# VectorE's side work in a gated MLP's tiles dealt out in other portions, and the weight loads of the projection phase moved to other steps

## The chip, the cores and the metric

One core of a Trainium2 chip runs the whole kernel. The metric is the device time of one execution in microseconds (us); the median of three runs is given. Engines are called by the profile's names: PE (TensorE; PEld is its weight load), DVE (VectorE), ACT (ScalarE), POOL (GpSimd) and SP (SyncE, which issues all DMAs of this kernel, in order).

## What is computed

A transformer block whose two branches run side by side on a layer norm of x (2048 tokens, width 640):

```python
def _B_ref(x, w_gate, w_up, w_down):
    g = jnp.einsum("bsd,df->bsf", x, w_gate)
    u = jnp.einsum("bsd,df->bsf", x, w_up)
    h = _gelu(g) * u
    return jnp.einsum("bsf,fd->bsd", h, w_down)

xn = _layernorm(x, axis=-1)
return x + _A_ref(xn, A_wqkv, A_wo) + _B_ref(xn, B_w_gate, B_w_up, B_w_down)
```

`_A_ref` is attention with 32 heads of 20 and a sliding window of 256, then a product with wo. The MLP's inner width is 1728. All is float32.

## The kernel before, in words

**Precision.** A float32 operand is split into a high part (a rounded copy, made by ACT) and a low part (raw minus high, made by DVE or POOL). A product takes three matmuls: high by high, low by high, high by low.

**Phases.** Layer norm and first projections; attention with the first MLP tiles filled in between (to about 656 us); the *gate phase* (to about 857 us); the *last phase* (to the end), in which h (1728 columns) and the attention output (640) are multiplied by w_down and wo, stacked as nine "quads" of 256 rows.

**Gate phase.** The inner width is cut into tiles f of 128 columns. Tiles f=6 to f=12 are done here, each in two passes of `gate_up_pair` (p=0 for tokens 0 to 1023, p=1 for the rest). A pass computes gate and up by a scheme that saves a product (sums of inputs and of weights, four accumulators pa, pb, pc, pe, in PSUM). It has 54 matmuls: pa 6, pb 9, pa 6, pc 9, pe 6, pc 9, pe 9. The second part of pc may start only when DVE has added the first part to q (`add(qp, pc_, q)`, L846, the "first qp add"), and the second part of pe after `add(qp, pe_, qp)`. Then come the gelu, the products h2 and h1 (L878) and their stores to hd (L882). At four places of a pass, `more(0)` to `more(3)`, the pass runs functions that were hung in (`extra`): more(0) and more(1) stand on DVE between the add to g1 and the first qp add, more(2) after the second qp add, more(3) after the add to g2. The next tile's splits and sums (`w_tiles`, `w_sums`) are among them. `load_gu` (L528) loads the next weights into "wr", two buffers.

**Side work.** A list of 21 jobs is done beside this (`Job`, L935; list, L970 to L974), each one a load by SP, some DVE instructions (items) and a store by SP:
- r0 to r3: a reciprocal of the softmax sums (1 item);
- t0 to t8: sums and differences of the four parts of a weight quad, written to wtd for the last phase (4 items, tile "ats");
- o0a, o0b to o3a, o3b: attention output times those reciprocals (3 and 2 items, tile "ato").

`work(cap)` (L978) makes one *visit*: it runs up to cap items of the oldest job under way, if that job's load was asked for at least three visits ago; a job without items left is stored and dropped; then one new job is loaded if fewer than two are under way:

```python
while n and going and going[0][1] <= hook[0] - 3:
    ...
if len(going) < 2 and jobs:
    job = jobs.pop(0)
    job.load()
    going.append((job, hook[0]))
```

ats and ato tiles share the tag "at" with three buffers; a load into a buffer waits on SP for the store of the job that had it. The caps per place are written out by hand in the loop over f. In the last tile (f=12) a loop (`while jobs or going: work(1)()`, L1224) does what is left, ahead of the second pass. Then come the first loads of the last phase (`load_step`, L1011, and `fetch`, L902); the last pass itself has the splits of the first quads (`quad`) and steps (`split_step`, L1025) hung into it.

**Last phase.** 80 steps: eight blocks of 256 tokens by nine quads and an end piece "e" (the last 64 rows of w_down, tile w13). Step n issues the loads for step n+4 (tag "hr", four buffers), splits the inputs of step n+2 and does `prepare(n)`, then its matmuls (L1087). Steps 0 to 13 (all of block 0, and quads 0 to 3 of block 1) are plain: 24 matmuls, 8 for "e". From step 15 on a step has 21 matmuls and a costlier split (tile "ss"), and needs the quads' t parts as well: t4 to t8 at steps 15 to 19, t0 to t3 at steps 26 to 29. After the last step of a block `drain` (L1096) adds the banks to x on DVE and stores the output.

`prepare` follows a table `tasks`: at the step named there the quad's high part is made (ACT, `high_quad`), at the next step its low part (DVE, `low_quad`). `("b", q)` is the quad as it is, `("t", q)` its sums from wtd. The quads are staged in "stg", three buffers of 640 KB, by `fetch`; b0, b2 and b3 come through "wr" and b1 through "at". Before, the fetches follow each other in the table's order: b4 ahead of step 0, b5 and b6 at steps 0 and 1, and from step 2 on one wherever a low part has been made (its buffer is free then).

The order of instructions on PE, ACT, DVE and SP is as written here, in the last phase POOL's too.

Of the kernel before, what the change touches and what calls it, by code (L numbers as in the profile page):

```python
# [60 lines left out]
def block_kernel(ctx, tc, x, wqk, wv, wgu, wdo, wdl, out):  # L61
# [730 lines left out]
    def w_tiles(raws, pool, bufs):  # L792
        g, u = raws
        gu = split(pool, g, [128, KT, 128], "wq", nc.gpsimd, bufs)
        uh = pool.tile([128, KT, 128], F32R, name="wqh", tag="wqh", bufs=bufs)
        ul = pool.tile([128, KT, 128], F32R, name="wql", tag="wql", bufs=bufs)
        hi_lo(u[:, 2:5], uh[:, 2:5], ul[:, 2:5], nc.gpsimd)
        return gu, (uh, ul)

    def w_sums(raws, sums):  # L800
        g, u = raws
        r = {i: c2.tile([128, 3 if i == 4 else 2, 128], F32, name=f"sr{i}") for i in (1, 2, 3, 4)}

        def dve(o, i, j, op=OP.subtract):
            nc.vector.tensor_tensor(out=o, in0=i, in1=j, op=op)

        def a1():
            dve(r[1], u[:, L], u[:, U], OP.add)
            dve(r[2], r[1], g[:, L])

        def a2():
            dve(r[3], g[:, L], u[:, L])
            dve(r[4][:, L], g[:, U], r[2])
            dve(r[4][:, 2], g[:, 4], u[:, 4])

        def fin(*which):
            for i in which:
                sums[i] = [c2.tile(list(r[i].shape), F32R, name=f"s{i}{n}") for n in "hl"]
                nc.scalar.activation(sums[i][0], r[i], AF.Copy)
            for i in which:  # L820
                dve(sums[i][1], r[i], sums[i][0].bitcast(F32))

        return a1, a2, lambda: fin(2, 1), lambda: fin(3), lambda: fin(4)
# [75 lines left out]
    def four(t):  # L899
        return t.rearrange("p k (h n) -> p (k h) n", h=2)  # L900

    def fetch(kind, q, where="stg"):  # L902
        if where == "wr":
            ts = [wrp.tile([128, KT, 128], F32, name="wr", tag="wr").rearrange("p k m -> p (k m)") for _ in range(2)]
            for i, t in enumerate(ts):
                nc.sync.dma_start(t, wdo[q][:, i])
            staged[kind, q] = [(t.rearrange("p (h n) -> p h n", h=2), slice(2 * i, 2 * i + 2)) for i, t in enumerate(ts)]
            return
        pool, bufs = (rp3, 3) if where == "stg" else (cp, 3)
        t = pool.tile([128, 4, HD], F32, name="stg", tag=where, bufs=bufs)  # L910
        nc.sync.dma_start(t, four(wdo[q]) if kind == "b" else wtd[q])
        if kind == "t" and q in borrow:
            staged[kind, q] = [(t[:, i:i + 1], slice(i, i + 1)) for i in range(4)]
        else:
            staged[kind, q] = [(t, slice(0, 4))]
# [8 lines left out]
    def high_quad(kind, q):  # L924
        for raw, t, dst in parts(kind, q):
            nc.scalar.activation(t[:, 0, dst], raw, AF.Copy)

    def low_quad(kind, q):
        for raw, t, dst in parts(kind, q):
            sub(t[:, 1, dst], raw, t[:, 0, dst].bitcast(F32))  # L930

    def sub(o, i, j, op=OP.subtract):
        nc.vector.tensor_tensor(out=o, in0=i, in1=j, op=op)  # L933
# [36 lines left out]
    jobs = [Job("r", 0), Job("r", 1)]  # L970
# [4 lines left out]
    going = []  # L975
    hook = [0]

    def work(cap):  # L978
        def fn():
            hook[0] += 1  # L980
            n = cap
            while n and going and going[0][1] <= hook[0] - 3:
                job = going[0][0]
                job.items.pop(0)()
                n -= 1
                if not job.items:
                    job.store()
                    going.pop(0)
            if len(going) < 2 and jobs:
                job = jobs.pop(0)  # L990
                job.load()
                going.append((job, hook[0]))
        return fn
# [17 lines left out]
    def load_step(n):  # L1011
        p, k = steps[n]
        c, t0 = p // 2, p % 2 * 256
        raw = raws[n] = cp.tile([128, 4, 128], F32, name="hr", tag="hr", bufs=4)
        flat = raw.rearrange("p a t -> p (a t)")
        if k == "e":
            for r in (0, 64):
                nc.sync.dma_start(flat[r:r + 64, 0:256], hd[NF - 1][c][:, t0:t0 + 256])
            return
        for i in range(2):  # L1020
            j = 2 * k + i
            src = hd[j][c] if j < NF - 1 else od[c][(j - NF + 1) * 128:(j - NF + 2) * 128]
            nc.sync.dma_start(flat[:, 256 * i:256 * i + 256], src[:, t0:t0 + 256])
# [153 lines left out]
    def split_later_xs(i, nxt=None):  # L1177
        def fn():
            split_xs(1, i, later[i])
            if nxt:  # L1180
                later[nxt] = load_xs(1, nxt)
        return fn
# [3 lines left out]
    def load_next(f):  # L1186
        def fn():
            raws_next[f] = load_gu(f)
        return fn

    raws_next = {NFA + 1: load_gu(NFA + 1)}
    for j, f in enumerate(range(NFA, NF - 1)):
        end = f + 1 == NF - 1
        first, second = {i: [] for i in range(4)}, {i: [] for i in range(4)}
        first[0] += carry
        if j == 0:
            first[0].append(split_later_xs(2, 4))
            first[2].append(split_later_xs(1))
            first[3].append(split_later_xs(3))
            second[0].append(split_later_xs(4))  # L1200
        if not end:
            nxt_w, sums = [], {}

            def next_tiles(j=j, raws=raws_next[f + 1]):
                nxt_w.append(w_tiles(raws, *pools[(len(sets) + j + 1) % 2]))

            first[3].append(next_tiles)
            items = w_sums(raws_next[f + 1], sums)
            second[2] += items[0:2]
            second[3].append(items[2])  # L1210
            carry = list(items[3:5])
            if f + 2 < NF - 1:
                second[3].append(load_next(f + 2))
        if j:
            for i, n in enumerate((0, 3, 1, 1)):
                first[i].append(work(n))
        if not end:
            for i, n in enumerate((1, 3, 1, 1) if j else (0, 0, 1, 1)):
                second[i].append(work(n))
        else:  # L1220
            fetch("b", 0, "wr")
        gate_up_pair(f, w, 0, first)
        if end:
            while jobs or going:  # L1224
                work(1)()
            for n in range(2):
                load_step(n)
            fetch("b", 1, "at")

            def quad(q):  # L1230
                high_quad("b", q)
                low_quad("b", q)

            second[0].append(lambda: quad(0))
            second[1].append(lambda: [split_step(0), fetch("b", 2, "wr"), load_step(2)])
            second[2].append(lambda: [split_step(1), quad(1), load_step(3)])
            second[3].append(lambda: [quad(2), fetch("b", 3, "wr")])
        stores = gate_up_pair(f, w, 1, second, end)
        if not end:
            w = nxt_w[0], sums  # L1240
# [9 lines left out]
    psn = p3.enter_context(tc.tile_pool(name="psn", bufs=1, space=PSUM, reuse_waits="tile"))  # L1250
    w13 = rp3.tile([128, 2, D], F32R, name="w13")

    tasks = {0: ("b", 3), 1: ("b", 4), 2: ("b", 5), 3: ("b", 6), 4: ("b", 7), 5: ("b", 8), 6: ("t", 4), 8: ("t", 5),
             9: ("t", 6), 10: ("t", 7), 11: ("t", 8), 12: ("t", 0), 13: ("t", 1), 20: ("t", 2), 22: ("t", 3)}
    queue = list(tasks.values())[1:]

    def prepare(n):
        if n in tasks:
            high_quad(*tasks[n])
        if n - 1 in tasks:  # L1260
            low_quad(*tasks[n - 1])
            if n > 1 and queue:
                fetch(*queue.pop(0))
        if n == 2:
            nc.scalar.activation(w13[:, 0], raw13, AF.Copy)
            sub(w13[:, 1], raw13, w13[:, 0].bitcast(F32))
        if n < 2:
            fetch(*queue.pop(0))

    fetch(*queue.pop(0))  # L1270
    for o, i in stores:
        nc.sync.dma_start(o, i)
    raw13 = rp3.tile([128, D], F32, name="xr", tag="xr")
# [2 lines left out]
    for n, (p, k) in enumerate(steps):  # L1276
        i = n % (NQD + 1)
# [62 lines left out]
```

## Time and profile before

| | us |
|---|---|
| median of three runs | 1107.2 (1105.37 to 1108.08) |
| the profiled execution | 1105.0 |
| its span | 1103.3 |
| PE busy | 1072.4 (97%) |
| DVE busy | 757.5 (69%) |
| ACT busy | 510.2 (46%) |
| POOL busy | 335.3 (30%) |
| first matmul of the gate phase's passes | about 671 |
| first matmul of the last phase | 856.7 |

The profile is of one execution. Busy time is that in which an engine executes; a matmul's end is modelled. Rows of a timeline give start, length, engine, line, operation, what is written and read, how many were merged, and in brackets the idle time ahead of it and what ended it. Rows of a table by stretch give for each engine busy time and count, then PE's granted clock, the busy share of the DMA engines and GB/s.

### The profile page before, as it was taken

The numbers are of one execution on the slowest core, as the hardware profiler recorded it, in microseconds if no ns is written. First come the engines' busy times: TensorE is split into PE (matmuls) and PEld (weight loads), VectorE is DVE, ScalarE is ACT, GpSimd is POOL, SyncE is SP. The second block draws the span as 40 slices with busy tenths as digits, with TensorE's granted clock in tenths as the row PEclk, the third lists the DMA queues.
The fourth block names the chain that finished last, engine by engine and source line by source line (L and its number), as shares of the span: only waits on it lengthen the run. The fifth ranks groups of instructions, "written<-read, shape, count | busy, mean of one in ns | idle before, by whom it ended". The sixth has DMA issues, their size and how long they took to land.

```text
span 1103.3 us, 20904 instructions
## 1 busy us (share of the span) xinstructions
PE 1072.4 (97%) x7253; PEld 858.0 (78%) x7253; DVE 757.5 (69%) x2089; ACT 510.2 (46%) x1031; POOL 335.3 (30%) x513
## 2 busy tenths in 40 slices
PE   8999999999999999999999999999995999999998
PEld 7877667666678767666666778888884999999998
DVE  7766667566666666666756636777775578888886
ACT  4434655556644556554554565233222454333332
POOL 5045624567626425644525241111110000000000
PEclk9999999999999999999999999999997999999999
DMA  5642342536443243434333225476567894343433
GB/s 203 193 135 90 104 145 86 151 110 199 131 116 94 78 119 101 135 128 128 108 112 97 63 84 186 154 243 218 208 231 272 269 302 153 108 138 118 138 123 113
DMA packets 96057, 162.30 MB, mean 147 GB/s; under 512 B 13248, under 2 KB 57920, under 8 KB 95952
## 3 DMA queue, kind: packets, MB, share of 16 engines
q1 hardware_dynamic: 95952, 160.97, 46.1%
q8 instruction: 57, 0.93, 0.4%
q14 instruction: 48, 0.39, 0.1%
HBM read 104.40 MB, written 56.23 MB: 146 GB/s over the span
## 4 chain that ended last, share of the span: by engine, by line
PE 77%; DVE 8%; DMA 7%; ACT 3%; issue 2%; SPq 1%; POOL 1%; DVEq 0%; ACTq 0%
PE ps_d L100 23%; PE ps_g L843 15%; PE ps L1087 11%; PE ps_o L515 7%; PE ps_e L493 7%; PE ps_m L441 7%; PE ps_v L100 5%; DMA hr<-hd 2%; DVE ss L933 2%; DMA hr<-od 1%; PE ps_g L100 1%; DVE junk L443 1%; DVE xr L1101 1%; ACT at L1047 1%; ACT P L495 1%
## 5 line engine op out<-in xcount | busy, mean ns | idle before, releaser
L443 DVE CUSTOM_DVE_ANT_0 junk<-ps_m,mask 128x384 bf16<-128x384 f32 (+2 forms) x512 | 271.7, 531 | 177.2 <-PE ps_m L441 135.9
L495 ACT ACTIVATE P<-ps_e 128x512 f32<-128x512 f32 (+2 forms) x384 | 197.7, 568 | 63.7 <-PE ps_e L493 57.5
L1087 PE MATMUL ps<-wb,at 128*128 128x320 f32 x999 | 156.6, 309 | 1.4 <-DVE xr L1101 1.2
L1087 PEld LDWEIGHTS ps<-wb,at 128*128 128x128 f32 x999 | 148.9, 188 | 2.3 <-issue 1.5
L501 POOL TENSOR_SCALAR_AFFINE_SELECT P<-P 128x512 f32<-128x512 f32 x128 | 84.5, 660 | 175.4 <-ACT P L495 168.5
L100 PE MATMUL ps_d<-xh,wql 128*128 128x512 f32 x430 | 129.2, 410 | 0.0
L100 PE MATMUL ps_d<-xl,wqh 128*128 128x512 f32 x430 | 128.6, 408 | 0.0
L100 PE MATMUL ps_d<-xh,wqh 128*128 128x512 f32 x430 | 128.5, 409 | 0.0
L441 PE MATMUL ps_m<-ks,qs 120*128 120x128 bf16 (+1 forms) x704 | 121.1, 275 | 3.6 <-DVE mx L443 1.9
L493 PE MATMUL ps_e<-qs,ks 122*128 122x128 bf16 (+2 forms) x704 | 113.0, 277 | 1.4 <-ACT P L495 0.8
L493 PEld LDWEIGHTS <-ks 122*128 122x128 bf16 x704 | 50.1, 98 | 54.8 <-issue 44.1
L1087 PE MATMUL ps<-wt,at 128*128 128x320 f32 x552 | 89.8, 310 | 0.8 <-DVE u L933 0.7
L100 PEld LDWEIGHTS ps_d<-xh,wql 128*128 128x128 f32 x430 | 77.9, 189 | 15.8 <-issue 2.3
L100 PEld LDWEIGHTS ps_d<-xl,wqh 128*128 128x128 f32 x430 | 78.2, 188 | 14.9 <-issue 0.6
L100 PEld LDWEIGHTS ps_d<-xh,wqh 128*128 128x128 f32 x430 | 77.8, 189 | 14.1 <-ACT xh L184 0.3
L441 PEld LDWEIGHTS <-qs 120*128 120x128 bf16 x704 | 62.1, 98 | 32.8 <-issue 14.1
L1087 PEld LDWEIGHTS ps<-wt,at 128*128 128x128 f32 x552 | 83.0, 188 | 1.8 <-DVE u L933 1.3
L515 PE MATMUL ps_o<-P,v 128*32 128x384 f32 (+2 forms) x1408 | 84.3, 386 | 0.0
L504 POOL TENSOR_SCALAR_AFFINE_SELECT P<-P 128x512 f32<-128x512 f32 x112 | 72.1, 654 | 37.3 <-ACT P L495 37.3
L515 PEld LDWEIGHTS ps_o<-P,v 128*32 128x32 f32 x1408 | 40.1, 110 | 39.5 <-issue 29.6
L224 POOL TENSOR_TENSOR pt<-r,pt 128x512 bf16<-128x512 f32 x40 | 46.7, 1169 | 79.3 <-ACT pt L223 79.2
L1047 ACT ACTIVATE at<-ss 128x512 fp32r<-128x512 f32 x59 | 37.2, 630 | 66.4 <-DVE ss L933 65.8
(179 smaller groups left out, 1700.2 us busy)
## 6 DMA issues: line engine op xcount, KB each, us to landing
hr<-hd SPq DMA_DIRECT2D x104, 128.0 KB
hd<-he SPq DMA_DIRECT2D x50, 256.0 KB
wr<-wgu SPq DMA_DIRECT2D x27, 320.0 KB
qs<-qd SPq DMA_DIRECT2D x32, 240.0 KB
ks<-kd SPq DMA_DIRECT2D x32, 240.0 KB
ats<-wdo SPq DMA_DIRECT2D x9, 640.0 KB
wtd<-ats SPq DMA_DIRECT2D x9, 640.0 KB
stg<-wtd SPq DMA_DIRECT2D x9, 640.0 KB
```

The costliest lines, as they stand in the source:

```text
L100: nc.tensor.matmul(ps, a(k), b(k), start=n == 0, stop=n == 3 * nk - 1)
L224: nc.gpsimd.tensor_tensor(out=pt[:, l, :], in0=r, in1=pt[:, 1, :], op=OP.subtract)
L441: nc.tensor.matmul(ps[:, lo:hi], lh, rhs, start=True, stop=True)
L443: nc.vector.tensor_tensor_reduce(out=junk[:, 0:n], in0=ps[:, 0:n], in1=mask[:, 384 - n:384], scale=1.0, scalar=NEG, op0=OP.add, op1=OP.max ...
L493: nc.tensor.matmul(ps[:, col:col + n], k[0:QROWS, j, kc:kc + 128], q[0:QROWS, j, q0:q0 + n], start=True, stop=True)
L495: nc.scalar.activation(pt[:, j, lo:hi], ps[:, lo:hi], AF.Exp, scale=SCALE)
L501: nc.gpsimd.affine_select(out=a, in_=a, pattern=[[0, 4], [1, 128]], compare_op=OP.is_ge, fill=0.0, base=0, channel_multiplier=-1)
L504: nc.gpsimd.affine_select(out=a, in_=a, pattern=[[0, 4], [-1, 128]], compare_op=OP.is_ge, fill=0.0, base=-1, channel_multiplier=1)
L515: nc.tensor.matmul(o[32 * j:32 * j + 32, q0:q0 + n], v[:, w0_:w0_ + 32], pt[:, j, col:col + n], start=i == 0, stop=i == len(todo) - 1, ski ...
L843: nc.tensor.matmul(ps, i, j, start=first and n == 0, stop=n == len(work) - 1, skip_group_check=True)
L1047: nc.scalar.activation(hi[:, 3:7], s, AF.Copy)
L1087: nc.tensor.matmul(ps[bank][:, 0:HD], a, b, start=bank not in begun, stop=final[p, bank] == n and j == len(work[bank]) - 1, skip_group_che ...
```

## The change

Three things. The caps of the visits are other ones; three jobs may be under way instead of two; and the loop that did the rest in the last tile is gone (an assertion stands there: nothing may be left). In the last phase the table `tasks` has most quads one or two steps later (t2 and t3 stay), and the fetches stand in a table of their own: b5 and b6 at steps 0 and 1 as before, each later one at three steps ahead of its task or when its buffer is free (one step after the task three fetches earlier), whichever is later. Worked out, the fetches stand at these steps:

| | b5 | b6 | b7 | b8 | t4 | t5 | t6 | t7 | t8 | t0 | t1 | t2 | t3 |
|---|---|---|---|---|---|---|---|---|---|---|---|---|---|
| before | 0 | 1 | 2 | 3 | 4 | 5 | 6 | 7 | 9 | 10 | 11 | 12 | 13 |
| after | 0 | 1 | 3 | 4 | 5 | 7 | 8 | 9 | 11 | 12 | 13 | 17 | 19 |

```diff
-            if len(going) < 2 and jobs:
+            if len(going) < 3 and jobs:
                 job = jobs.pop(0)
                 job.load()
                 going.append((job, hook[0]))
...
         if j:
-            for i, n in enumerate((0, 3, 1, 1)):
+            for i, n in enumerate((0, 3, 1, 2)):
                 first[i].append(work(n))
         if not end:
-            for i, n in enumerate((1, 3, 1, 1) if j else (0, 0, 1, 1)):
+            for i, n in enumerate((2, 3, 1, 1) if j else (0, 2, 1, 1)):
                 second[i].append(work(n))
         else:
             fetch("b", 0, "wr")
         gate_up_pair(f, w, 0, first)
         if end:
-            while jobs or going:
-                work(1)()
+            assert not jobs and not going
             for n in range(2):
                 load_step(n)
             fetch("b", 1, "at")
...
-    tasks = {0: ("b", 3), 1: ("b", 4), 2: ("b", 5), 3: ("b", 6), 4: ("b", 7), 5: ("b", 8), 6: ("t", 4), 8: ("t", 5),
-             9: ("t", 6), 10: ("t", 7), 11: ("t", 8), 12: ("t", 0), 13: ("t", 1), 20: ("t", 2), 22: ("t", 3)}
-    queue = list(tasks.values())[1:]
+    tasks = {0: ("b", 3), 2: ("b", 4), 3: ("b", 5), 4: ("b", 6), 5: ("b", 7), 6: ("b", 8), 8: ("t", 4), 10: ("t", 5),
+             11: ("t", 6), 12: ("t", 7), 13: ("t", 8), 14: ("t", 0), 15: ("t", 1), 20: ("t", 2), 22: ("t", 3)}
+    late = list(tasks)[2:]
+    fetch_at, ready = {}, [1] + [n + 1 for n in list(tasks)[1:]]
+    for i, n in enumerate(late):
+        fetch_at[i if i < 2 else max(n - 3, ready[i - 1])] = tasks[n]
 
     def prepare(n):
         if n in tasks:
             high_quad(*tasks[n])
         if n - 1 in tasks:
             low_quad(*tasks[n - 1])
-            if n > 1 and queue:
-                fetch(*queue.pop(0))
...
-        if n < 2:
-            fetch(*queue.pop(0))
-
-    fetch(*queue.pop(0))
+        if n in fetch_at:
+            fetch(*fetch_at[n])
+
+    fetch("b", 4)
```

## The prediction

> **What bounds the kernel now.** I read the page first, then the waits of PE, then the chain that ended last, then the stretch around the one large gap engine by engine.
>
> ```profile
> span 1103.3 us, 20904 instructions
> ...
> PE   8999999999999999999999999999995999999998
> ...
> PEclk9999999999999999999999999999997999999999
> ```
>
> TensorE is the bound: its row reads 9 in every slice but three. Slice 31 (827 to 855 us) has 5 and a granted clock of 7. The waits of PE name it:
>
> ```profile
> PE ps_g L843 <- DVE qp L846: 12.8, 1, 12.8
> ```
>
> That one wait is larger than all others of PE together. The chain through it (start, length, what):
>
> ```profile
> 832.10 3.72 DMA wtd<-ats
> 835.88 3.71 DMA ats<-wdo
> ...
> 850.64 4.19 PE ps_g L843 x9
> ```
>
> and VectorE in that time:
>
> ```profile
> 832.16 1.90 DVE L933 TENSOR_TENSOR ato<-ato,rb 128x512 f32<-128x512 f32 x3
> ...
> 838.28 1.29 DVE L933 TENSOR_TENSOR ato<-ato,rb 128x512 f32<-128x512 f32 x2 [4.22 <-DMA ato<-od]
> ...
> 841.86 2.07 DVE L933 TENSOR_TENSOR ats<-ats 128x320 f32<-128x320 f32 x4 [2.29 <-issue]
> ```
>
> Between the two passes of the last tile (f=12) the loop at L1224 empties what is left of the jobs: I count one item of t2, five of o3, four of t3, ten in all. VectorE takes its instructions in order, so the adds that PE needs (L846) stand behind ten items, of which six wait for loads that were issued only then. The load of t3 itself waited for the store of t2 (its buffer). That is the stall: not VectorE's work, but loads asked for too late.
>
> **The change part by part.**
>
> *The loop in the last tile goes.* Counted by the rule in work(): before, the visits offer 62 items and 50 are taken by the end of the last tile's first pass, because only two jobs are under way and one must be three visits old. After, with three under way and 75 offered, all 60 are done at the first visit of the second pass of f=11; the last tile has none. So the 12.8 us of waiting go, and a loss of clock behind them:
>
> ```profile
> 847.00:852.00 5.00, 1.36 (x3) 1.17 (x4) 2.58 (x4) 1.27 (x3) 0.00 (x0) 0.50 0.95 305
> ...
> 867.00:872.00 5.00, 3.96 (x27) 3.69 (x26) 1.92 (x2) 2.38 (x5) 0.00 (x0) 1.00 0.96 359
> ```
>
> ```profile
> 726.47 0.69 DVE L846 TENSOR_TENSOR qp<-ps_g,q 128x512 f32<-128x512 f32 x1
> ...
> 824.39 0.69 DVE L846 TENSOR_TENSOR qp<-ps_g,q 128x512 f32<-128x512 f32 x1 [0.58 <-PE ps_g L843]
> ...
> 856.72 14.24 PE L1087 MATMUL ps<-wb,at 128*128 128x320 f32 x96
> ```
>
> In the stretches the third number from the end is the granted clock: 0.50 behind the long gap, 1.00 around a gap of about 1 us. A pass is 54 matmuls; its first qp add comes at 726.47 and, eight passes on, at 824.39, so 12.24 us a pass, 0.227 a matmul. The 18 matmuls left behind the gap took 850.64 to 856.72 = 6.08 us instead of 4.08: 2.0 more. Together **-14.8**.
>
> *The items in other portions.* Nearly all 60 items now lie in f=7 to f=11, up to five ahead of the first qp add, where before there were at most four:
>
> ```profile
> 700.00 0.95 DVE L944 RECIPROCAL rc<-rc 128x128 f32<-128x128 f32 x1
> ...
> 711.45 1.93 DVE L933 TENSOR_TENSOR ats<-ats 128x320 f32<-128x320 f32 x4
> ...
> 724.48 1.89 DVE L933 TENSOR_TENSOR ato<-ato,rb 128x512 f32<-128x512 f32 x3
> ...
> 825.25 0.41 PEld L843 LDWEIGHTS ps_g<-xh,s4h 128*128 128x128 f32 x2
> ```
>
> An item costs 0.48 (ats), 0.64 (ato) or 0.95 (reciprocal). The add may be late by little: the one at 824.39 ends at 825.08 and PE's dependent load starts at 825.25. Second passes fit: the fullest (f=7: three ats, two ato, 2.7 us from 711.45) ends at 714.2, when its add is due (726.47 less one pass). First passes are tighter: three ato at f=8 ended at 726.37, 0.10 ahead of the add; after, f=8 has ato, reciprocal, ats (2.1 us), f=9 two ato and a reciprocal (2.2), f=10 and f=11 three ato as before, each behind larger items at visits 2 and 3 of the pass ahead. I work out lateness of 0.1 to 0.4 us in four passes. Bounds: nothing, or one ato uncovered in each of four (2.6); near the tight row, **+0.5**.
>
> *Three loads under way* share the three "at" buffers, so that seven times a load stands on SP right behind the store that frees its buffer, 3.72 us (the wtd store above). Behind it on SP stand, at worst, the next tile's weights:
>
> ```profile
> 766.90 0.82 SPq L528 DMA_DIRECT2D wr<-wgu  x2
> ...
> 780.02 0.72 ACT L92 ACTIVATE wqh<-wr 128x640 fp32r<-128x640 f32 x1
> ```
>
> They are issued 13.1 us ahead of their first reader; with 3.7 for landing 9.4 are spare. Two such pairs in one pass (second passes of f=9, f=10) block SP for 7.4 us, less than that. I take 0; the other end, all seven uncovered, is 26 (a rival below).
>
> *The last pass without its pause.* The pause also covered the first loads of the last phase.
>
> ```profile
> 831.08 0.93 SPq L882 DMA_DIRECT2D hd<-he  x2
> ...
> 844.38 2.44 SPq L1023 DMA_DIRECT2D hr<-hd  x4
> 846.87 0.43 SPq L911 DMA_DIRECT2D stg<-wdo  x1
> ...
> 862.12 1.66 SPq L1018 DMA_DIRECT2D hr<-hd  x2
> ```
>
> That was SP's queue, and this is ScalarE:
>
> ```profile
> 834.52 0.60 ACT L862 ACTIVATE q<-ps_g 128x512 f32<-128x512 f32 x1 [1.49 <-PE ps_g L843]
> ...
> 848.63 0.63 ACT L1038 ACTIVATE at<-hr 128x512 fp32r<-128x512 f32 x1 [3.43 <-DMA hr<-hd]
> 851.98 1.27 ACT L926 ACTIVATE wb<-stg 128x1280 fp32r<-128x1280 f32 x1 [1.31 <-DMA stg<-wdo]
> ...
> 868.78 0.42 ACT L1031 ACTIVATE he<-hr 128x256 fp32r<-128x256 f32 x1 [1.70 <-DMA hr<-hd]
> ```
>
> Now the hr loads go out at 832.0, right behind the hd stores. If they take as long as here (844.38 to 848.63, 4.25 us) they are there at 836.3; ScalarE's copy 0.63, VectorE's subtraction 0.69, then the qp add 0.69 make 838.3. PE ran dry at 837.8 (850.64 less 12.8), and its next matmul was due 0.1 earlier. So a wait of 0.6; or of 0.2 when the load is faster and ScalarE's order alone sets it (q from 834.52 and the gelu behind it, 0.6 each, end at 835.75). The upper end is a load as slow as the one from 862.12 to 868.78, 6.7 us: 840.7, a wait of 3.0. I take **+0.6**, by the nearest row. [...]
>
> *First steps of the last phase.* What follows is late against PE, because PE no longer waits:
>
> ```profile
> 872.08 0.41 PE L1087 MATMUL ps<-w,he 128*128 128x320 f32 x1 [1.12 <-ACT w L1265]
> 872.94 1.29 PE L1087 MATMUL ps<-w,he 128*128 128x320 f32 x7 [0.45 <-DVE w L933]
> ...
> 893.06 14.31 PE L1087 MATMUL ps<-wb,at 128*128 128x320 f32 x96 [1.23 <-DVE xr L1101]
> ```
>
> and from SP and ScalarE:
>
> ```profile
> 857.72 1.07 SPq L906 DMA_DIRECT2D wr<-wdo  x2
> ...
> 870.13 1.27 ACT L926 ACTIVATE wb<-stg 128x1280 fp32r<-128x1280 f32 x1 [0.92 <-DMA stg<-wdo]
> 871.31 0.72 ACT L1265 ACTIVATE w<-xr 128x640 fp32r<-128x640 f32 x1
> ```
>
> b1 would be issued at 834.4 and with 5.1 us (846.87 to 851.98) reach ScalarE at 839.5; copy, subtraction, g2 add, gelu, copy and half a subtraction of b2 (1.3 + 1.5 + 0.7 + 0.6 + 0.7 + 0.8) free b3's buffer at 845, 2.6 us behind step 0 (837.7 + 4.08 + 0.6 = 842.4), where it is 1.0 now. So b3, and w13 at step 4, come 1.5 us later against PE. In return w13's copy no longer stands behind b5's (870.13 to 871.31; b4, landed earlier, takes that place): -0.9. **+0.5** on the 1.57 us of waiting at step 4; ends -1.57 and +2.
>
> *Weight loads spread out.* To step 11 ten quads are fetched instead of twelve, 1.3 MB less in front of the hr loads while the DMA share is 0.96. The 1.23 us at 893.06 come from the drain's first add, which VectorE reaches late, behind a split whose hr load it awaits; I give half back, **-0.6** (0 to -1.23). The price: t7, t8, t0, t1 are now converted at steps 13 to 16, where only t0 and t1 were.
>
> ```profile
> 903.28 0.29 DVE L933 TENSOR_TENSOR ss<-hr 128x128 f32<-128x128 f32 x1 [0.51 <-DMA hr<-hd]
> ...
> 905.61 1.48 DVE L933 TENSOR_TENSOR wt<-stg,wt 128x1280 fp32r<-128x1280 f32 x1
> ...
> 911.79 0.29 DVE L933 TENSOR_TENSOR ss<-hr 128x128 f32<-128x128 f32 x1 [0.96 <-DMA hr<-od]
> ...
> 923.42 1.68 DVE L1101 TENSOR_TENSOR xr<-ps,xr 128x320 f32<-128x320 f32 x4
> ```
>
> From 911.79 to the drain at 923.42 VectorE does five splits, 2.33 us each, without a gap. Two more subtractions of 1.5 to 1.7 make 3.2; the 0.96 of DMA wait pays part, so the drain is at most 2.3 late if VectorE still starts step 13 at 903.28, and not late if earlier hr loads let it start 2 us sooner. **+0.6**.
>
> Sum: -14.8 + 0.5 + 0.6 + 0.5 - 0.6 + 0.6 = **-13.2**. The profiled execution took 1105.0 us (span 1103.3, 1.7 around it): 1091.8. The median shown is 2.2 above it, so on its scale 1107.2 - 13.2 = **1094.0**.
>
> **Rivals.**
> *The last pass still waits.* For: its hr loads now follow the stores by nothing. With the 6.7 us load: 3.0 instead of 0.6, 1096.4; if so long a gap also cost clock, up to 2.0 more, 1098.4. [...] The trace has 12.8 us with loss and 1.1 without, and nothing between.
> *All covered.* The waits at 872 and 893 vanish too: -14.8 + 0.2 - 1.57 - 1.23 = -17.4, 1089.8. For: less DMA traffic; against: b3's chain.
> *SP's queue becomes the bound (slower).* Seven store-then-load pairs at 3.72 are 26 us; were all exposed to PE through late weights of the next tile, 1094.0 + 26 = 1120. It begins to cost where the blocks of a pass exceed 9.4 us, and is a loss from about 13 us exposed. Against it: two pairs make 7.4.
> *The change moves the stall instead of removing it* (items that wait for their loads in f=8 to f=11): shortest lead of a load on its first item that I count is 8 to 10 us, against 3.7 to 7.4 needed. If so, about 1107.
>
> **How the numbers follow.** Forecast 0.63, last pass still waits 0.15, all covered 0.13, SP's queue 0.05, stall moved 0.04. The range 1089.5 to 1099.5 holds the first three and leaves the rest out. A measurement of this kernel tells about 0.3% (3.3 us) from no change: faster 0.91, within 0.03, slower 0.06.
>
> **What would show it.** Right: no wait of PE on L846 above 1 us, granted clock 1.00 throughout 820 to 860, the first L1087 matmul near 842.5, ats and ato rows only up to about 810. Wrong: waits of PE on L846 in f=8 to f=11 adding up to over 3 us, L528 issues later than 9 us, or PE waits on DVE xr around 910 of over 2 us.

## The result, and the profile after

| | before | after |
|---|---|---|
| median (lowest to highest), us | 1107.64 (1105.37 to 1108.71, 4 runs) | 1094.07 (1092.35 to 1095.3, 4 runs) |
| profiled execution, its span | 1105.0, 1103.3 | 1093.39, 1091.7 |

The ratio is 0.9879, 95% interval 0.9857 to 0.9901: faster by 1.2%. The forecast was 1094.0. The page of the kernel after:

```profile
span 1091.7 us, 20910 instructions
...
PE   8999999999999999999999999999999999999998
...
PEclk9999999999999999999999999999999999999999
```

The 5 in slice 31 and the 7 of its clock are gone. The waits of PE (line waited for: us in total, times, longest), from the top:

```profile
PE ps_t L176 <- DVE xi L159: 3.9, 4, 1.5
PE ps_m L441 <- DVE mx L443: 2.0, 6, 0.7
PE ps_m L441 <- DMA sd<-ob: 1.5, 1, 1.5
PE ps_u L387 <- DVE warm L384: 1.2, 1, 1.2
PE ps L1087 <- ACT w L1265: 1.1, 1, 1.1
PE ps L1087 <- DVE u L933: 1.1, 2, 0.7
```

The 12.8 us on L846 headed this list before. Now L846 isn't in it, and what is left in the last phase are single waits of at most 1.15 us. The chain that ended last no longer goes through the side work's wtd and ats in the last tile. It goes through the first loads of the last phase:

```profile
835.18 5.09 DMA stg<-wdo
846.99 7.06 DMA stg<-wdo
854.07 3.08 DMA hr<-hd
```

The last pass, on SP, ScalarE and VectorE:

```profile
831.83 0.93 SPq L882 DMA_DIRECT2D hd<-he  x2
833.17 1.97 SPq L1023 DMA_DIRECT2D hr<-hd  x4
```

```profile
835.77 0.62 ACT L863 ACTIVATE hr<-hr 128x512 f32<-128x512 f32 x1
836.37 0.63 ACT L1038 ACTIVATE at<-hr 128x512 fp32r<-128x512 f32 x1
```

```profile
837.03 0.69 DVE L933 TENSOR_TENSOR at<-hr,at 128x512 fp32r<-128x512 f32 x1 [0.91 <-ACT at L1038]
837.64 0.68 DVE L846 TENSOR_TENSOR qp<-ps_g,q 128x512 f32<-128x512 f32 x1
```

The loads stand right behind the stores, and ScalarE's copy of what they brought (836.37) starts when the gelu ahead of it is done, with no wait for a DMA in its brackets. The first qp add ends at 838.32, and no matmul of PE waited for it (its weight load did, 0.17 us).

**Where the time went.** Three rows cut both traces at the same work: the first DVE product of the gate phase, the first matmul of the last phase (856.72 before, 842.60 after), and the end pieces "e" of blocks 1 and 2, which are the rows ps<-w,he. Before:

```profile
662.58 0.69 DVE L765 TENSOR_TENSOR he<-ps_g,gs 64x512 f32<-64x512 f32 x1 [1.07 <-ACT gs L764]
```

```profile
907.21 1.34 PE L1087 MATMUL ps<-w,he 128*128 128x320 f32 x8
936.89 1.34 PE L1087 MATMUL ps<-w,he 128*128 128x320 f32 x8
```

After:

```profile
663.33 0.69 DVE L765 TENSOR_TENSOR he<-ps_g,gs 64x512 f32<-64x512 f32 x1 [1.07 <-ACT gs L764]
```

```profile
842.60 11.27 PE L1087 MATMUL ps<-wb,at 128*128 128x320 f32 x74
...
859.13 0.41 PE L1087 MATMUL ps<-w,he 128*128 128x320 f32 x1 [1.15 <-ACT w L1265]
859.99 1.57 PE L1087 MATMUL ps<-w,he 128*128 128x320 f32 x7 [0.45 <-DVE w L933]
...
894.54 1.34 PE L1087 MATMUL ps<-w,he 128*128 128x320 f32 x8
925.31 1.34 PE L1087 MATMUL ps<-w,he 128*128 128x320 f32 x8
```

| us | before | after | difference |
|---|---|---|---|
| ahead of the gate phase (no edit there) | 662.58 | 663.33 | +0.75 |
| gate phase | 194.14 | 179.27 | -14.87 |
| last phase, first matmul to e of block 1 | 50.49 | 51.94 | +1.45 |
| e of block 1 to e of block 2 | 29.68 | 30.77 | +1.09 |
| the rest of the span | 166.41 | 166.39 | 0.0 |

The gate phase gained 14.9 us, and the first two blocks of the last phase gave 2.5 back. In the first of these stretches a loss appears that before had not at this place (busy time and count of PE, PEld, DVE, ACT, POOL, then granted clock, DMA share, GB/s):

```profile
856.00:860.00 4.00, 2.40 (x16) 1.92 (x14) 1.31 (x3) 3.12 (x5) 0.00 (x0) 1.00 0.91 341
860.00:864.00 4.00, 4.00 (x16) 3.70 (x17) 3.95 (x4) 2.56 (x3) 0.00 (x0) 0.60 0.78 232
864.00:868.00 4.00, 4.00 (x28) 4.00 (x28) 2.09 (x2) 1.22 (x2) 0.00 (x0) 0.97 0.93 304
```

From 860 to 864 PE did 16 matmuls where 29 fit, at a clock of 0.60, behind gaps of 0.33, 1.15 and 0.45 us. By whole microseconds from 860 on the clock is 0.91, 0.50, 0.50, 0.50 and 0.89: about 3.4 us at half speed. What that cost is read from the rows: from step 4's second matmul to e1 after takes 34.55 us (from 859.99), before 33.04 (from 872.94, without a gap of 1.23 at the first drain), so 1.5 us. Before, the same place had gaps of 1.12 and 0.45 and kept its clock:

```profile
870.00:874.00 4.00, 2.43 (x15) 1.94 (x14) 3.12 (x4) 3.87 (x5) 0.00 (x0) 1.00 0.86 291
874.00:878.00 4.00, 4.00 (x29) 4.00 (x28) 2.89 (x3) 1.50 (x2) 0.00 (x0) 1.00 0.90 278
```

A second loss there is seen only in part in PE's rows. The 96 matmuls of steps 0 to 3 last from 842.60 to 857.99, 15.39 us, where before they take 14.24. At step 3 the weight loads (PEld) stand idle for 0.26, 0.55 and 0.29 us, until 853.46, 854.20 and 854.93: for the low part of that step's input and for the two low parts of b3, which VectorE makes late because ScalarE had to wait for b3's load:

```profile
851.43 0.74 ACT L926 ACTIVATE wb<-wr 128x640 fp32r<-128x640 f32 x1 [1.87 <-DMA wr<-wdo]
```

```profile
853.33 1.56 DVE L933 TENSOR_TENSOR wb<-wr,wb 128x640 fp32r<-128x640 f32 x2
```

### The profile page after: what moved, and what is told of

It reads as the page before. It is cut to its first block, busy times and chain, and to the rows that moved or that the text cites. A ratio compares the mean times of both kernels' runs of the same rounds, so it can differ in the third digit from the quotient of the medians.

```text
span 1091.7 us, 20910 instructions
## 1 busy us (share of the span) xinstructions
PE 1073.2 (98%) x7253; PEld 857.9 (79%) x7253; DVE 757.4 (69%) x2089; ACT 509.7 (47%) x1031; POOL 335.3 (31%) x513
## 4 chain that ended last, share of the span: by engine, by line
PE 78%; DVE 9%; DMA 5%; ACT 3%; issue 3%; SPq 1%; POOL 1%; DVEq 0%; ACTq 0%
PE ps_d L100 23%; PE ps_g L843 15%; PE ps L1087 12%; PE ps_o L515 7%; PE ps_e L493 7%; PE ps_m L441 6%; PE ps_v L100 6%; DVE ss L933 2%; DMA hr<-hd 1%; PE ps_g L100 1%; DVE junk L443 1%; DMA stg<-wdo 1%; DVE xr L1101 1%; ACT at L1047 1%; ACT P L495 1%
## 5 line engine op out<-in xcount | busy, mean ns | idle before, releaser
L1087 PE MATMUL ps<-wb,at 128*128 128x320 f32 x999 | 159.1, 312 | 0.6 <-DVE wb L933 0.3
L100 PEld LDWEIGHTS ps_d<-xl,wqh 128*128 128x128 f32 x430 | 78.3, 188 | 14.8 <-issue 0.6
```

The lines of the kernel that those rows point to most:

```text
L100: nc.tensor.matmul(ps, a(k), b(k), start=n == 0, stop=n == 3 * nk - 1)
L1087: nc.tensor.matmul(ps[bank][:, 0:HD], a, b, start=bank not in begun, stop=final[p, bank] == n and j == len(work[bank]) - 1, skip_group_che ...
```

## The experiments

All stretches below are cut as in the table above; "to e1" is the first matmul of the last phase to e of block 1, "e1 to e2" the next one. The part ahead of the gate phase lies between 662.6 and 667.9 in these traces, though nothing there was edited, so stretches say more than single spans. Each ratio is to the kernel before, run beside it. In pool_low the lines behind L931 are numbered three higher, and w13's copy is at L1261 to L1266 depending on the kernel.

| kernel | runs: median (range) | ratio, 95% interval | gate | to e1 | e1 to e2 |
|---|---|---|---|---|---|
| gate_only | 1094.85 (1092.98 to 1097.15) | 0.9890 (0.9873 to 0.9907) | 179.28 | 53.47 | 29.25 |
| table_only | 1105.82 (1104.31 to 1108.24) | 0.9988 (0.9977 to 0.9998) | 193.96 | 48.84 | 30.25 |
| three_only | 1100.07 (1098.5 to 1101.65) | 0.9936 (0.9919 to 0.9952) | 182.50 | 53.62 | 28.91 |
| caps_only | 1097.31 (1096.08 to 1101.57) | 0.9918 (0.9897 to 0.9938) | 183.30 | 53.71 | 29.78 |
| b1_early | 1091.8 (1090.58 to 1092.39) | 0.9862 (0.9843 to 0.9881) | 179.27 | 50.66 | 31.16 |
| w13_early | 1096.18 (1094.35 to 1096.88) | 0.9902 (0.9887 to 0.9917) | 179.22 | 54.95 | 31.30 |
| both_new | 1092.79 (1089.63 to 1093.37) | 0.9869 (0.9850 to 0.9888) | 179.22 | 48.39 | 31.16 |
| both_old | 1094.2 (1090.19 to 1094.49) | 0.9877 (0.9858 to 0.9896) | 179.62 | 52.25 | 29.26 |
| b1_w13 | 1091.58 (1090.87 to 1093.16) | 0.9848 (0.9821 to 0.9875) | 179.87 | 49.78 | 32.31 |
| pool_low | 1095.33 (1094.28 to 1097.05) | 0.9887 (0.9869 to 0.9904) | 180.02 | 49.47 | 34.33 |
| t01_late | 1094.38 (1092.37 to 1096.37) | 0.9870 (0.9850 to 0.9891) | 179.63 | 49.59 | 28.96 |

The theory: the gain is the stall of the last tile and nothing else; what is given back comes from the first steps of the last phase, whose loads the stall had covered, and from VectorE's way to the second drain. The rivals: the new table is what gains, or three loads under way (or the new caps) would have done by themselves.

### The halves alone: gate_only and table_only

gate_only is the kernel after with the old `tasks`, `queue` and `prepare`; table_only is the kernel before with the new ones.

> The other caps, three jobs under way and no loop in the last tile, but the last phase's table and fetches as before. Theory (the loop's stall and its clock loss are the whole gain; the new table only moves waits of a microsecond about): 12.5 to 15.5 us faster than before, no wait of PE on L846 above 1 us, PE waiting 1.5 to 2.5 us for w13 at step 4 and 1 to 1.5 us at the first drain, none of 1 us at the second. Rival (the spread loads are needed, since without the pause the last phase is short of DMA): only 8 to 11 us faster, with 2 to 5 us more PE waits in steps 3 to 12 than in the changed kernel.

> Only the new table and fetches of the last phase; gate phase as before with its loop. Theory: within 1.5 us of before; the 12.8 us wait of PE on L846 stays, the w13 wait shrinks by about 0.9 us and the second drain costs about 1 us more. Rival (the spread loads bring a part of the gain): 2 to 5 us faster.

gate_only has after's gate phase to 0.01 us, and after's time within the spread. Two of its waits came out otherwise than expected: 2.67 us at step 4, where 1.5 to 2.5 was said, and only 0.20 at the first drain, where 1 to 1.5 was. PE comes to that drain late itself. table_only keeps the stall:

```profile
PE ps_g L843 <- DVE qp L846: 12.3, 1, 12.3
```

So the gain is the gate phase's. The table's part is a trade: against gate_only, after is 1.53 better to e1 and 1.52 worse from e1 to e2. With the stall still there (table_only against before) it is 1.65 better and 0.57 worse, and the runs show 0.1%, just told from nothing. In gate_only PE waits longer at step 4, and the loss of clock behind it is longer too:

```profile
860.41 0.64 PE L1087 MATMUL ps<-w,he 128*128 128x320 f32 x1 [2.67 <-ACT w L1264]
```

```profile
860.00:864.00 4.00, 3.36 (x11) 3.02 (x12) 3.61 (x5) 2.86 (x5) 0.00 (x0) 0.50 0.86 256
864.00:868.00 4.00, 4.00 (x21) 4.00 (x20) 1.22 (x1) 0.96 (x1) 0.00 (x0) 0.65 0.99 298
```

### The gate phase's two parts alone: three_only and caps_only

Both are the kernel before, with its loop and its old table.

```diff
# three_only
-            if len(going) < 2 and jobs:
+            if len(going) < 3 and jobs:
# caps_only
-            for i, n in enumerate((0, 3, 1, 1)):
+            for i, n in enumerate((0, 3, 1, 2)):
-            for i, n in enumerate((1, 3, 1, 1) if j else (0, 0, 1, 1)):
+            for i, n in enumerate((2, 3, 1, 1) if j else (0, 2, 1, 1)):
```

> Before, with three jobs under way instead of two, nothing else; the loop stays, and by my count it has one item left (the last of t3), whose load was asked for a tile earlier. Theory (late loads are the stall, not the items): 12 to 15 us faster than before. Rival (the stall is VectorE's amount of work in the gate phase, which the new portions change): under 5 us faster.

> Before, with the new caps only, two jobs under way; by my count the loop has the four items of t3 left, whose load was asked for in the last tile's first pass, about 8 us ahead. Theory: 11 to 14.5 us faster, a PE wait on L846 of 0.5 to 2.5 us left. Rival (only the third load under way does it): under 8 us faster, a wait of 5 us or more left.

Each alone brings most of the gate phase's gain, and neither all of it. In the runs both missed their expectation: three_only gained 0.64% where 12 to 15 us (1.1 to 1.4%) were expected, caps_only 0.82% where 11 to 14.5 us (1.0 to 1.3%) were. Their gate phases are 11.6 and 10.8 us shorter, and both give 3.1 to 3.2 back to e1, by a wait at step 4 (2.63 and 2.02) with a lower clock behind it (0.67 from 868 to 872 in three_only, 0.57 from 864 to 868 in caps_only). three_only's waits of PE on L846 are two, 2.7 us together, and behind the first stands the very queue that the prediction had as its slower rival. SP and VectorE of three_only in f=11:

```profile
802.57 0.38 SPq L967 DMA_DIRECT2D od<-ato  x1
...
809.01 0.38 SPq L958 DMA_DIRECT2D ato<-od  x1
809.49 0.91 SPq L882 DMA_DIRECT2D hd<-he  x2
```

```profile
815.34 0.69 DVE L878 TENSOR_TENSOR he<-qp,hr 128x512 f32<-128x512 f32 x1 [4.07 <-DMA hd<-he]
...
819.23 0.69 DVE L846 TENSOR_TENSOR qp<-ps_g,q 128x512 f32<-128x512 f32 x1
```

A side-work load waits on SP for the store of its buffer, the last 3.1 us of it alone, until 809.01. The stores of the h that VectorE had finished at 802.0, in the pass before, stand behind it and go out at 809.49. VectorE needs their buffer for the next products and waits 4.07 us for them; the qp add behind it is late and PE waits 1.27. The second wait, 1.41, is in the last pass: the one item that is left starts at 838.43, its store goes out at 838.96 and the hr loads behind it only at 839.46. In caps_only the pass of the last tile has t3's four items in it. They cost nothing by themselves (2.06 us from 832.09). But the store of their result (SP, 834.17) stands ahead of the hr loads (834.60), and VectorE waits for these:

```profile
839.32 0.69 DVE L933 TENSOR_TENSOR at<-hr,at 128x512 fp32r<-128x512 f32 x1 [3.11 <-DMA hr<-hd]
```

```profile
840.67 1.22 PE L843 MATMUL ps_g<-xh,s4h 128*128 128x512 f32 x2 [2.27 <-DVE qp L846]
```

That is the prediction's rival "the last pass still waits", near its size (2.27 where 3.0 was said, and a granted clock of 0.57 from 840 to 844), in a kernel that leaves one job over. In before, three_only and caps_only, each with items left in the last tile, the wait is there; in gate_only and after, with an empty list, it is gone.

### The first steps of the last phase: b1_early, w13_early, both_new, both_old

All on the kernel after. b1_early issues b1's fetch ahead of the last tile's first pass instead of behind it. w13_early takes w13 ahead of the quads and b4's fetch behind the loads for step 4. both_new does both, both_old does both with the old table.

```diff
# b1_early
             fetch("b", 0, "wr")
+            fetch("b", 1, "at")
         gate_up_pair(f, w, 0, first)
...
-            fetch("b", 1, "at")
# w13_early, in prepare(n); w13's two lines stand ahead of the quads
+        if n == 0:
+            fetch("b", 4)
...
-    fetch("b", 4)
```

> The changed kernel, with b1 fetched ahead of the last tile's first pass instead of behind it. Theory (the last phase lost 2.5 us because its first loads are asked for too late against PE, each link waiting for the one before: b1, the subtraction of b2, b3's buffer, the stores, the loads of step 4): ScalarE's wait of 2.3 us for b1 goes, b3 is asked for 1 to 1.5 us earlier, the wait for w13 shrinks from 1.6 us to under 0.7, no clock is lost there; 1.5 to 3.5 us faster than the changed kernel. Rival (DMA throughput, not the time of asking, sets when step 4's inputs land): no change, within 0.7 us.

> The changed kernel, with b4's fetch behind step 4's loads instead of ahead of the stores, and w13's copy and subtraction ahead of b4's. Theory: 640 KB less ahead of w13 and the hr load of step 4, which land 2 us earlier or more; the wait at step 4 falls from 1.6 us to under 0.5 and the half clock behind it (1.65 us) goes: 2 to 3.5 us faster than the changed kernel. Rival (the wait only moves to b4 at step 5 or to b3 at step 3): under 1 us faster, the same sum of PE waits in steps 3 to 6.

> Both of the above. Theory: no wait of PE above 0.5 us from step 0 to the first drain, clock 1.00 throughout; 2.5 to 4 us faster than the changed kernel, some 16 to 18 faster than before. Rival (the last phase is bound by its DMA volume): as the better of the two alone or worse.

> The same two edits with the old table of the last phase. Theory (the new table costs about 1 us at the second drain, since VectorE has two more subtractions there, and gives nothing that the two edits don't): 0 to 1.1 us faster than with the new table, second drain's PE waits 0.4 instead of 1.1. Rival (spread loads matter once PE no longer pauses): 1 us or more slower than with the new table, by waits for hr loads in steps 4 to 12.

b1_early gains 1.28 to e1 (ratio 0.9862 against 0.9879, the intervals overlap). b3 goes out 1.57 us behind the first matmul of the last phase (843.65) instead of 3.27 (845.87 in after), the three waits at step 3 are gone, and e of block 0 begins 15.39 us after that matmul instead of 16.53 (15.36 before). The wait at step 4, which was expected to go, stays: the piece he lands at 855.22, and b4's copy of 1.25 us stands between it and w13's. w13_early has the longest last phase of all (252.67 us against after's 249.10), though in the runs its interval overlaps after's: b4 and the input of step 5 behind it are late instead, PE waits 2.79 us at step 5, and the clock is at 0.50 until 868. both_new has the shortest way to e1 of all, with one gap of 0.99 us and a clock of 1.00. But 2.5 to 4 us over after were expected of it, and its median is only 1.3 better; the profiled execution is the fastest of its four (1089.63, the others 1092.51 to 1093.37). both_old shows what the new table is for once b1 is early. With the old one PE waits at the first drain, which is the wait that the prediction gave half back:

```profile
PE ps L1087 <- DVE xr L1101: 2.5, 1, 2.5
```

But from e1 to e2 it is again the other way round, 29.26 against 31.16: of the 3.86 us that the new table saves in block 0, half is paid at the second drain. In the runs the two can't be told apart.

### The second drain: b1_w13, pool_low, t01_late

b1_w13 is b1_early with w13's two lines ahead of the quads, and b4's fetch where the change has it. The other two build on it: pool_low does three late subtractions on POOL, t01_late puts t0 and t1 behind the drain, and t2 and t3 a little later, so that the third block has all four.

```diff
# pool_low, in low_quad
+            if kind == "t" and q in (8, 0, 1):
+                nc.gpsimd.tensor_tensor(out=t[:, 1, dst], in0=raw, in1=t[:, 0, dst].bitcast(F32), op=OP.subtract)
# t01_late
-             11: ("t", 6), 12: ("t", 7), 13: ("t", 8), 14: ("t", 0), 15: ("t", 1), 20: ("t", 2), 22: ("t", 3)}
+             11: ("t", 6), 12: ("t", 7), 13: ("t", 8), 19: ("t", 0), 21: ("t", 1), 23: ("t", 2), 25: ("t", 3)}
```

> The changed kernel with b1 fetched ahead of the last tile's first pass, and in prepare(2) w13's copy (ScalarE) and subtraction (VectorE) ahead of b4's; b4's fetch stays where the change has it. Theory (the first steps of the last phase lose 1.57 us of waiting at step 4 because w13's copy stands behind b4's 1.27 us copy, and 1.7 us of clock behind it): with b1 early the piece he lands at 855.2, w13's copy no longer stands behind b4's, the wait at step 4 falls from 1.2 + 0.4 to under 0.4, PE's granted clock stays at 1.00 from 856 to 866 in the profile, and block 0 is some 1.5 to 3 us shorter: last phase 246 to 247, 1089 to 1091 in the runs. Rival (the wait only moves, as it did with w13 early alone): b4's copy, 0.7 later on ScalarE, and its low part on VectorE become late for step 5, PE waits 1 us or more on them, and the last phase stays at 248 to 249, 1091.5 to 1094.

> The kernel with b1 early and w13's copy ahead, and the low parts of t8, t0 and t1 (steps 14 to 16) on POOL, which does nothing in the last phase, instead of VectorE. Theory (with the new table VectorE comes late to the second drain, because these 128x1280 subtractions of 1.48 us lie in its last seven splits): VectorE reaches the drain's first add 3 to 4 us earlier against the first step, the wait of PE on m (1.49 us) goes, and from the e piece of block 1 to that of block 2 it takes 29.2 to 29.7 us instead of 32.3; last phase 246 to 246.5, 1088.5 to 1090 in the runs. Rival (the loads hr set VectorE's pace there, the subtractions only fill its waits): VectorE waits for hr instead, and the stretch stays at 31 to 32 us. Second rival: POOL's subtraction, an estimated 3.2 us from its 1.62 us for 128x640, makes VectorE's rows longer while it runs or frees the staging buffer so late that t2's or t1's load slips; then rows of at<-ss over 0.75 us show it.

> The kernel with b1 early and w13's copy ahead, and t0 and t1 behind the second drain: tasks at steps 19 and 21, t2 and t3 at 23 and 25 (t0 to t3 are needed from step 26 on). Theory: two subtractions of 1.48 us fewer ahead of the second drain, VectorE reaches it about 3 us earlier, no wait on m; from the e piece of block 1 to that of block 2 29.2 to 29.7 us instead of 32.3. The third block then has four subtractions in place of two; its stretch stays at 30.1 us if VectorE has the room (nine splits of 2.33, the drain's 5.5, four times 1.48: 32.4 us of about 30.8, so it may lose up to 1.5 at the third drain). Last phase 246 to 248, 1088.5 to 1091. Rival (hr loads set VectorE's pace): the second stretch stays at 31 to 32.

In b1_w13 both expectations hold in part. At step 4 the gaps are 0.20 and 0.44, the clock stays at 1.00, and b4 costs 0.99 a step later, as the rival said; the median lies in the rival's range. It reaches e1 2.16 us sooner than after does, and then PE waits at the second drain:

```profile
860.96 31.70 PE L1087 MATMUL ps<-wb,at 128*128 128x320 f32 x214 [0.99 <-DVE wb L933]
910.73 1.51 PE L1087 MATMUL ps<-wb,at 128*128 128x320 f32 x6 [1.49 <-ACT m L1114]
914.59 0.70 PE L1087 MATMUL ps<-wt,at 128*128 128x320 f32 x3 [0.72 <-DVE u L933]
```

From e1 to e2 it takes 32.31: 1.54 of the 2.16 are given back there, because VectorE sets that point and PE only comes to it earlier. t01_late shows it: with two subtractions of 1.48 us out of the way that stretch is 28.96, the shortest but one of the runs, and the wait on m there is gone. The next stretch (e of block 2 to e of block 3) pays: 34.44 instead of 30.13, a loss of 4.3 where at most 1.5 was expected, so the kernel as a whole gains nothing.

```profile
894.73 1.33 PE L1087 MATMUL ps<-w,he 128*128 128x320 f32 x8
923.69 1.34 PE L1087 MATMUL ps<-w,he 128*128 128x320 f32 x8
958.13 1.34 PE L1087 MATMUL ps<-w,he 128*128 128x320 f32 x8
```

```profile
943.62 1.51 PE L1087 MATMUL ps<-wb,at 128*128 128x320 f32 x6 [1.97 <-ACT m L1114]
```

So the two subtractions can be moved from one drain to the next, and whichever block has it is late. pool_low fell by its second rival, and by more than that said. POOL, then VectorE, in pool_low:

```profile
898.68 3.05 POOL L931 TENSOR_TENSOR wt<-stg,wt 128x1280 fp32r<-128x1280 f32 x1 [3.19 <-ACT wt L926]
```

```profile
898.61 0.29 DVE L936 TENSOR_TENSOR ss<-hr 128x128 f32<-128x128 f32 x1
898.82 3.06 DVE L936 TENSOR_TENSOR ss<-hr,ss 128x128 f32<-128x128 f32 x1
```

The VectorE instruction that meets POOL's takes 3.06 us instead of 0.29: it ends 0.15 us after POOL's. The other two go the same way (3.26 and 3.02 us on VectorE). Handing over 1.48 us of VectorE's work cost VectorE about 2.8 us.

The fastest of all are b1_early and b1_w13, 1091.8 and 1091.58 in the runs. They beat the kernel before, and after by some 2 us in the median; the intervals of the ratios (b1_w13 to 0.9875, after from 0.9857) still overlap. Their traces don't bear the 2 us out: from the first product of the gate phase to the end they take 427.9 and 428.7 us, after 428.4. That they are faster than after is not shown.

## Why the prediction was right, point by point

**The loop goes, -14.8.** Right, in both its parts. The gate phase is 14.87 us shorter, with nothing for two terms beside it. The last side-work item starts at 810.13, the wait of 12.8 is gone, and the 18 matmuls behind the first qp add take 4.12 us (838.48 to 842.60) instead of 6.08, at a clock of 1.00 from 820 to 860.

**Items in other portions, +0.5.** Measured 0.0: from 699.34 to 821.74 ten passes of after take 122.40 us, as ten of before do from 698.59 to 820.99. No first qp add was late enough for PE.

**SP's store-then-load pairs, 0.** Right for after. Two pairs lie in the second passes of f=9 and f=10, and the weights behind them went out at 772.16 and 799.10 instead of 766.90 and 791.38, by 5.3 and 7.7 us (0.75 of it from ahead of the gate phase), under the 9.4 that were spare. The rival built on them was sound in its mechanism: three_only shows it, through the stores of h and not through the weights.

**The last pass without its pause, +0.6.** Measured 0. The loads, issued at 833.17, were there by 836.37, in at most 3.2 us where 4.25 was taken, and ScalarE's order set the copy, as in the case that the prediction priced at 0.2. The 4.25 was a misreading: it counts from the start of four issues that keep SP busy for 2.44 us. In the chain of before the load that the copy waited for takes 2.25 us, from 846.39 on.

**First steps of the last phase, +0.5 for the waits.** Measured about +2.7, beyond the +2 that the step allowed. The waits at step 4 are 1.60 (1.15 and 0.45), as good as the 1.57 before. What failed is two things. The prediction saw b3 come late, but priced it at step 4 alone: b3 went out 3.27 us behind the first matmul instead of the 2.6 worked out, and cost 1.15 at step 3. And the step priced no clock: it was at half speed for about 3.4 us, which cost 1.5. The prediction knew such a loss only for the long gap and as a rival in the last pass.

**First drain, -0.6.** Its gap of 1.23 is gone entirely, the outer end of that term. That the new table can do this shows in both_old (a gap of 2.51) against both_new (none). In after alone it isn't separated from PE's own lateness, since gate_only, with the old table and PE late, has a gap of only 0.20 there. With the step before, 1.15 + 0.03 + 1.5 - 1.23 = 1.45, which is all that the stretch to e1 lost.

**Second drain, +0.6.** Measured +1.09, inside the 2.3 allowed. The reason given, VectorE behind the later subtractions, is what t01_late bears out. VectorE's first add of that drain starts 16.94 us behind e1 (911.48) instead of 16.21 (923.42). The wait of 0.96 for a load is gone, as hoped, but it doesn't pay for the whole.

So the gate phase came out 1.2 better than its three terms (-13.7) and the last phase 2.0 worse than its own (+0.5); two errors of opposite sign. The mechanism of the gain was right; that the sum came out within 0.1 us is luck. That the medians differ by 13.6 and the cut traces from the gate phase on by 12.3 is within the spread of single executions.

## What to carry to other kernels

When a stall goes, everything that was quietly loaded in its shade comes due earlier: look at the first loads of the next stage, and price not only their wait but the clock that may be lost behind it (in after 1.5 us, behind waits of 1.15 and 0.45). Side work in an in-order queue has to be done ahead of the last place where the queue's own loads start; a deeper queue or larger portions alone got half to two thirds of this gain in the runs, because one job left over or one blocked load stood in front of the rest (PE waited 2.27 us in caps_only, 1.27 and 1.41 in three_only). And where an engine is full around a fixed point (VectorE around each drain here), moving its work in time moves the wait, and a helper engine helps only if the two can run side by side: in pool_low a VectorE subtraction beside one of POOL took 3.06 us instead of 0.29.

## What the runs showed of the hardware

**The clock fell behind every gap of 1.97 us or more, and behind some shorter ones.** Every gap of PE in the last tile and the last phase of 1.97 us or more was followed by a granted clock of 0.50 to 0.73 over the next 4 us or so (1.97 in t01_late, 2.02 and 2.27 in caps_only, 2.51 in both_old, 2.63 in three_only, 2.67 in gate_only, 2.79 in w13_early and 12.8 in before). Behind the 12.3 of table_only a single 128x512 matmul took 0.63 us (at 854.76) where 0.39 is the length ahead of the gap. The largest without such a loss was 1.70, in pool_low. Two short gaps in a row went either way: 1.12 and 0.45 in before and 0.20, 0.44 and 0.99 in b1_w13 kept 1.00; 1.15 and 0.44 in b1_early and 0.33, 1.15 and 0.45 in after halved it. Worked out from the granted clock by stretch, taken as 0.50 while it is low, the slow time is an estimated 3.4 us in after, b1_early, three_only, both_old and t01_late and 6.8 in gate_only and w13_early. What sets these lengths, and why some pairs of short gaps cost clock and others none, no run here shows.

**Beside POOL's subtractions in pool_low, VectorE's instructions lasted as long as POOL's.** Each of POOL's three subtractions there (3.30, 3.05 and 2.99 us) met one instruction of VectorE that lasted about as long, 3.26, 3.06 and 3.02 us; the second and third of these take 0.28 or 0.29 us elsewhere in that trace. No run here shows the cause.
